# Rows 2 to 6 loaded in four 32-partition transfers, rows 0 to 6 stored in two 64-partition transfers

## The chip, the cores and the metric

The kernel runs on one core of a Trainium2 chip. The metric is device time in microseconds (us) of one execution; lower is better. Three runs of the kernel before gave 107.68, 107.85 and 108.42 us, so the median is 107.85 us. The core has five engines: PE (TensorE, matmul), DVE (VectorE), ACT (ScalarE), POOL (GpSimd) and SP (SyncE, which here only issues transfers and waits). Sixteen DMA engines move data between HBM, the memory outside the core, and SBUF, the core's working memory of 128 partitions.

## What is computed

The reference is windowed attention followed by a low-rank mixture of experts on the attention's output:

```
q, k, v: (8, 8, 576, 64) float32      # batch, heads, positions, head dim
scores = q k^T / 8
heads 0-3 keep 0 <= i-j < 32
heads 4-7 keep 0 <= i-j < 128 and (i-j) % 4 == 0
x = softmax(scores) v                 # then laid out as (8*576, 512)
logits = x @ w_gate                   # 512 -> 8 experts, the best two are taken, softmax of the two
out = x + sum over those two e of  w_e * (x @ A[e]) @ B[e]     # rank 16
```

All inputs and the output are float32; the kernel computes the matmuls in bfloat16 with float32 sums.

## The kernel before

A "row" here is one batch entry, r from 0 to 7. Each row has two groups g of four heads: the plain window and the dilated one.

**Data of a row.** One input slot `IN[r % 4]` holds q, k and v of a row in bfloat16 over 128 partitions; there are four slots, so row r+4 can only be loaded once row r's scores (operations `S...`) and value products (`V...`) have read their slot. Heads are packed in pairs, one of a pair in partitions 0 to 63 (half 0), the other in 64 to 127 (half 1). Each half of a row is a run of `ROW` = 6948 elements per partition, and the two halves start at different columns of the slot, with zeros in the rest. The result of a row is `X[r]`, 128 partitions x 2304 float32; each row has its own `X`, never reused.

**Loads.** They are issued from POOL (function `load`, line 248), because the transfer also turns float32 in HBM into bfloat16 in SBUF: an element is read as 4 bytes and written as 2. Every load names one half, that is 64 partitions. Rows 0, 1 and 7 come in several pieces so that their work can start early; rows 2 to 6 are one operation `L2` ... `L6` of two transfers, 64 partitions x 6948 elements each, and everything that uses the row waits for both:

```
a = load(f"L{r}", r, [(0, 0, ROW), (1, 2 * VB, ROW)], used.get(r - SLOTS, []))
```

**Work of a row.** For each group: scores and their mask on PE (`S`), exponentials on ACT (`E`, line 312), products with v on PE (`V`), reciprocal and division on DVE (`R` line 347, `N` line 350, which writes `X`), a bfloat16 copy on POOL (`B`, line 355). Then the experts: transposes on PE (`T`, `U`), copies, gate logits and first factor (`Z`), the top-two gates on DVE and ACT (`m0` to `g2`), scaling on POOL (`gz`, line 434), transposes (`G`), the second factor on PE (`D`) and its addition to `X` on DVE (`A`, lines 469 and 484).

**Stores.** They are issued from SP. Rows 0 to 6 are one transfer each of 128 partitions x 2304 float32 (line 496, operations `O0` to `O6`); row 7 goes in two transfers of 128 partitions x 1152, one per group (line 500, `O71` and `O70`). Each store waits for its row's additions and for a piece of row 7's load.

**Order.** The order of all operations is written out by hand in the text `PLAN`; each engine executes its own operations in that order. Semaphore waits are derived from the dependencies. An operation of several transfers has one semaphore, which counts 16 per transfer, and those who need it wait for all. Two rules are added for stores (lines 102 to 106): every store but the first waits for load `L71`, which is the last load to be issued, and a store of rows 0 to 6 waits for the store before the previous one, so that two are in flight:

```
if name[0] == "O":
    o.deps = o.deps + ([f"L{B - 1}1"] if stores else [])
    if int(name[1]) < B - 1:
        o.deps = o.deps + stores[-2:-1]
    stores.append(name)
```

The stores stand in the plan in the order `O1`, `O0`, `O3`, `O2`, `O4`, `O5`, `O6`, `O71`, `O70`.

The functions that the diff touches, with line numbers as the profile uses them:

Of the kernel before, what the change touches and what calls it, by code (L numbers as in the profile page):

```python
# [25 lines left out]
VB = 2 * NB * VW  # L26
ROW = 2 * (QK + VB)
SW = ROW + 2 * VB
XG = 1152
SLOTS = 4  # L30
# [44 lines left out]
class Program:  # L75
# [5 lines left out]
    def add(self, name, eng, work, emit, deps=(), bank=None):  # L81
        assert name not in self.ops, name
        o = Op(name, eng, work, emit, [d for d in deps if d is not None], bank)
        self.ops[name] = o
        if bank is not None:
            bank.users.append(name)
        return name
# [73 lines left out]
def program(nc=None, qkv=None, aw=None, bt=None, con=None, out=None):  # L161
    scale = 1.0 / float(D) ** 0.5
    pg = Program()
    add = pg.add

    def sb(name, shape, dt):
        return nc.alloc_sbuf_tensor(name, shape, dt) if nc is not None else None

    IN = [sb(f"in{i}", [128, SW], BF) for i in range(SLOTS)]
    X = [sb(f"x{r}", [128, 2 * XG], FP) for r in range(B)]  # L170
# [23 lines left out]
    def half(a):  # L194
        return slice(64 * a, 64 * a + 64)
# [45 lines left out]
    qk_ready, v_ready = {}, {}  # L241
    used = {}

    def load(name, r, parts, deps):

        def emit():
            return [
                nc.gpsimd.dma_start(  # L248
                    out=IN[r % SLOTS][half(a), at : at + n],
                    in_=qkv[r, a, :, at - 2 * VB * a : at - 2 * VB * a + n],  # L250
                )
                for a, at, n in parts
            ]

        return add(name, "POOL", ("dma", sum(64 for _ in parts), sum(4 * n for _, _, n in parts) // len(parts), len(parts)), emit, deps)

    def loads(r):
        if r == 0:
            for g in range(2):
                a = load(f"Lk{r}{g}", r, [(h, QK_AT[h][g], QK) for h in range(2)], [])  # L260
                b = load(f"Lv{r}{g}", r, [(h, V_AT[h][g], VB) for h in range(2)], [])
                qk_ready[r, g], v_ready[r, g] = [a], [b]
        elif r in (1, B - 1):
            free = used.get(r - SLOTS, [])
            a = load(f"L{r}0", r, [(0, VB, VB + QK), (1, 2 * VB + QK, VB + QK)], free)
            qk = [(0, 2 * VB + QK, QK), (1, 2 * VB, QK)]
            v = [(0, 0, VB), (1, ROW + VB, VB)]
            qk_ready[r, 0] = v_ready[r, 0] = [a]
            if r == 1:
                qk_ready[r, 1] = v_ready[r, 1] = [load(f"L{r}1", r, qk + v, free)]  # L270
            else:
                qk_ready[r, 1], v_ready[r, 1] = [load(f"L{r}1", r, qk, free)], [load(f"L{r}2", r, v, free)]
        else:
            a = load(f"L{r}", r, [(0, 0, ROW), (1, 2 * VB, ROW)], used.get(r - SLOTS, []))
            for g in range(2):
                qk_ready[r, g] = v_ready[r, g] = [a]

# [210 lines left out]
    for r in range(B):  # L488
        loads(r)
        for g in range(2):  # L490
            attention(r, g)
        used[r] = [f"S{p}{r}{g}" for p in range(2) for g in range(2)] + [f"V{r}{g}" for g in range(2)]
        adapters(r)
    for r in range(B):
        if r < B - 1:
            add(f"O{r}", "SP", ("dma", 128, 9216), lambda r=r: [nc.sync.dma_start(out=out[r], in_=X[r][:, :])],
                [f"A{r}{n}" for n in range(3)] + [f"L{B - 1}0"])
        else:
            for g in range(2):
                add(f"O{r}{g}", "SP", ("dma", 128, 4608), lambda r=r, g=g: [nc.sync.dma_start(  # L500
                    out=out[r][:, XG * g : XG * g + XG], in_=X[r][:, XG * g : XG * g + XG])],
                    [f"A{r}{g}", f"A{r}2", f"L{B - 1}0"])
# [92 lines left out]
```

## Time and profile before

| | us |
|---|---|
| median of three runs | 107.85 |
| the profiled execution's own time | 108.36 |
| its span, first to last instruction | 106.6 |
| PE busy | 83.0 |
| DVE busy | 73.2 |
| ACT busy | 56.7 |
| POOL busy | 44.6 |

The transfers wrote 24.68 MB at their destinations, a mean of 232 GB/s over the span. The page divides the span into 40 slices of 2.67 us; for each it gives the busy share of every engine in tenths, the granted clock of PE, the mean busy share of the 16 DMA engines and the rate. A rate counts the bytes as written; since the row loads read 4 bytes for 2 written, their reading rate is twice the rate shown. "Issue to landing" is the time from the instruction that issues a transfer until its semaphore shows it done, so it includes the wait behind other transfers. Sizes in KB are 1024 bytes; rates in GB/s are 10^9 bytes per second.

### The profile page before, as it was taken

The page shows a single profiled execution, that of the slowest core. Times are in us where ns is not written, and L with a number is a line of the kernel's source. Part 1 is how long each engine was busy: PE and PEld are TensorE (multiplying, and loading weights), DVE is VectorE, ACT ScalarE, POOL GpSimd, SP SyncE. Part 2 cuts the span into 40 slices and gives each one's busy share as a digit, 9 for nine tenths or more (in the row PEclk, how much of TensorE's full clock was granted, in tenths as well). Part 3 has the DMA queues.
Part 4 walks back from the last instruction along what each step waited for, and adds up shares of the span by engine and source line. Part 5 has one row for each costly group of instructions (what it writes and reads, how often), then busy time and mean ns, then how long its engine had stood idle before and what let it go on. Part 6 is the DMA issues. An engine that isn't in the chain of part 4 may idle for free.

```text
span 106.6 us, 3605 instructions
## 1 busy us (share of the span) xinstructions
PE 83.0 (78%) x1599; PEld 60.4 (57%) x1603; DVE 73.2 (69%) x167; ACT 56.7 (53%) x83; POOL 44.6 (42%) x59
## 2 busy tenths in 40 slices
PE   4999986799868768979739729999999998852700
PEld 1334662585647545868539517988887896621300
DVE  6772088187691794968319804899999799998630
ACT  0126603478529716765936918638896956650100
POOL 6999028307180177106643790047350945300000
PEclk9999999999999999999999995899999999998555
DMA  2999999999898999999999999936982999993982
GB/s 45 345 204 203 224 210 209 225 221 236 188 246 188 230 197 224 236 203 219 204 167 209 199 187 182 201 79 266 234 164 106 384 397 374 412 401 159 415 360 111
DMA packets 4142, 24.68 MB, mean 232 GB/s; under 512 B 672, under 2 KB 800, under 8 KB 2592
## 3 DMA queue, kind: packets, MB, share of 16 engines
q0 software_dynamic: 2400, 14.23, 66.3%
q1 hardware_dynamic: 1584, 9.95, 22.8%
q10 hardware_dynamic: 144, 0.28, 0.8%
q8 instruction: 12, 0.20, 0.7%
q14 instruction: 2, 0.02, 0.0%
HBM read 29.25 MB, written 9.44 MB: 363 GB/s over the span
## 4 chain that ended last, share of the span: by engine, by line
PE 31%; DMA 28%; DVE 19%; POOL 8%; issue 7%; ACT 2%; DVEq 1%; POOLq 0%
DMA in<-in_qkv_dram 28%; PE ps L204 26%; POOL in L248 8%; DVE x L469 6%; DVE x L350 5%; PE ps L371 4%; ACT p L312 1%; DVE x L484 1%; DVEq L586 1%; DVE gc L447 1%; DVE g L428 1%; PE ps L443 1%; DVE rec L347 1%; PE ps L390 1%; DVE gz L434 1%
## 5 line engine op out<-in xcount | busy, mean ns | idle before, releaser
L355 POOL CAST xb<-x 128x1152 bf16<-128x1152 f32 x16 | 19.7, 1229 | 31.5 <-DVE x L350 31.5
L312 ACT ACTIVATE p<-ps 128x960 bf16<-128x960 f32 (+1 forms) x32 | 27.5, 892 | 9.7 <-PE ps L204 9.6
L204 PE MATMUL ps<-in,p 128*64 128x130 bf16 (+1 forms) x416 | 21.4, 221 | 4.0 <-issue 3.0
L469 DVE TENSOR_TENSOR x<-x,ps 128x1024 f32<-128x1024 f32 x16 | 19.4, 1216 | 6.4 <-PE ps L204 6.3
L350 DVE TENSOR_TENSOR x<-ps,rec 128x1152 f32<-128x1152 f32 x16 | 21.7, 1354 | 0.4
L204 PEld LDWEIGHTS ps<-in,p 128*64 128x64 bf16 (+1 forms) x416 | 17.4, 104 | 7.5 <-issue 3.5
L248 POOL DMA_DIRECT2D in<-in_qkv_dram x30 | 15.9, 584 | 0.8 <-POOLq L577 0.8
L434 POOL TENSOR_TENSOR gz<-zs,g 128x640 bf16<-128x640 f32 x7 | 8.9, 1275 | 14.5 <-DVE g L428 14.3
L204 PE MATMUL ps<-in 64*64 64x96 bf16 (+1 forms) x576 | 12.0, 205 | 2.6 <-issue 2.6
L204 PEld LDWEIGHTS ps<-in 64*64 64x64 bf16 x576 | 11.1, 110 | 5.1 <-issue 3.0
L204 PE MATMUL ps<-con 64*64 64x384 bf16 (+1 forms) x128 | 12.2, 372 | 1.8 <-DMA in<-in_qkv_dram 1.3
L204 PE MATMUL ps<-warm 128*128 128x512 bf16 x39 | 11.6, 446 | 2.1 <-DVE warm L208 1.5
L383 ACT COPY xt<-ps 128x1024 bf16<-128x1024 bf16 x8 | 8.1, 1016 | 7.7 <-PE ps L371 7.7
L347 DVE RECIPROCAL rec<-ps 128x18 f32<-128x18 f32 x16 | 4.2, 266 | 11.4 <-PE ps L204 11.4
L371 PE MATMUL ps<-con,xb 128*128 128x128 bf16 x128 | 10.1, 225 | 1.5 <-POOL xb L355 1.4
L204 PE MATMUL ps<-aw,xt 128*128 128x136 bf16 x160 | 11.2, 223 | 0.0
L380 ACT COPY xt<-ps 128x1024 bf16<-128x1024 bf16 x8 | 8.1, 1014 | 5.2 <-PE ps L371 5.1
L415 ACT COPY zs<-ps 128x408 f32<-128x408 f32 (+1 forms) x16 | 6.9, 446 | 6.6 <-PE ps L204 6.5
L204 PEld LDWEIGHTS ps<-aw,xt 128*128 128x128 bf16 x160 | 9.6, 98 | 0.6
L371 PEld LDWEIGHTS ps<-con,xb 128*128 128x128 bf16 x128 | 8.0, 101 | 3.1 <-POOL xb L355 2.7
L239 DVE MEMSET in<- 64x1170 uint32 x8 | 8.3, 1033 | 2.1 <-issue 2.1
L449 ACT COPY gn<-ps 128x576 bf16<-128x576 bf16 x8 | 5.1, 640 | 7.1 <-DVE gc L447 6.9
(33 smaller groups left out, 70.6 us busy)
## 6 DMA issues: line engine op xcount, KB each, us to landing
in<-in_qkv_dram POOLq DMA_DIRECT2D x10, 868.5 KB, 15.8
out_dram<-x SPq DMA_DIRECT2D x7, 1152.0 KB, 5.7
in<-in_qkv_dram POOLq DMA_DIRECT2D x8, 288.0 KB, 7.1
in<-in_qkv_dram POOLq DMA_DIRECT2D x4, 434.2 KB, 9.9
in<-in_qkv_dram POOLq DMA_DIRECT2D x8, 146.2 KB, 8.2
out_dram<-x SPq DMA_DIRECT2D x2, 576.0 KB, 2.9
awf<-in_aw_dram ACTq DMA_DIRECT2D x1, 272.0 KB, 3.7
btf<-in_bt_dram SPq DMA_DIRECT2D x1, 256.0 KB, 3.7
```

The costliest lines, as they stand in the source:

```text
L204: return nc.tensor.matmul(o, lhsT=lhsT, rhs=rhs, start=start, stop=stop, skip_group_check=True)
L239: add(f"vz{i}{a}", "DVE", ("zero", 1170), lambda i=i, a=a: [nc.vector.memset(zeros(i, a), 0)])
L248: nc.gpsimd.dma_start(out=IN[r % SLOTS][half(a), at : at + n], in_=qkv[r, a, :, at - 2 * VB * a : at - 2 * VB * a + n],)
L312: return [nc.scalar.activation(p[:, :, :].rearrange("p h (s c) -> p h s c", c=PER)[:, :, b0 : b0 + nb, 0:SEG], PS[:, k.at : k.at + 2, 0 : ...
L350: nm = add(f"N{tag}", "DVE", ("el", XG), lambda: [nc.vector.tensor_tensor(X[r][:, XG * g : XG * g + XG].rearrange("p (b i n) -> p b i n", ...
L355: add(f"B{tag}", "POOL", ("el", XG), lambda: [nc.gpsimd.tensor_copy(XB[r % 2][:, g], X[r][:, XG * g : XG * g + XG])], [nm] + ([f"T{r - 2}{ ...
L371: nc.tensor.transpose(tp[:, 512 * j + 128 * u : 512 * j + 128 * u + 128], xb[:, g, 256 * u + 128 * j : 256 * u + 128 * j + 128], ident())
L380: return [nc.scalar.copy(xt[:, 0:2, 0:S].rearrange("p j (c i) -> p j c i", c=C)[:, :, :, 0:128], tp.rearrange("p j (i c) -> p j c i", c=C))]
L383: return [nc.scalar.copy(xt[:, 2:4, 0:512], tp)]
L415: zc.append(add(f"Y{st}{r}", "ACT", ("el", len(us) * ZW), lambda us=us, k=k: [nc.scalar.copy(zs[:, us[0] : us[-1] + 1].rearrange("p u n -> ...
L434: return [en.tensor_tensor(GZ[i][:, :, :].rearrange("p u (e r) -> p u e r", e=E), zs[:, :, 0:ER].rearrange("p u (e r) -> p u e r", e=E), G ...
L469: return [nc.vector.tensor_tensor(v, v, PS[:, k.at : k.at + 2].rearrange("p b n -> p (b n)"), ALU.add)]
```

## The change

The function that emits loads takes a width `cut` in partitions. With 32, each half of a row is loaded by two transfers, of partitions 0 to 31 and 32 to 63 of the half. This is used for rows 2 to 6 only, so ten transfers become twenty. Each store of rows 0 to 6 becomes two transfers, partitions 0 to 63 and 64 to 127; seven transfers become fourteen. The two stores of row 7 stay as they are. Bytes, waits and the order of operations on every engine stay the same; the pieces of one operation are issued one after the other and share its semaphore.

```
-    def load(name, r, parts, deps):
+    def load(name, r, parts, deps, cut=64):
 
         def emit():
             return [
                 nc.gpsimd.dma_start(
-                    out=IN[r % SLOTS][half(a), at : at + n],
-                    in_=qkv[r, a, :, at - 2 * VB * a : at - 2 * VB * a + n],
+                    out=IN[r % SLOTS][64 * a + p : 64 * a + p + cut, at : at + n],
+                    in_=qkv[r, a, p : p + cut, at - 2 * VB * a : at - 2 * VB * a + n],
                 )
-                for a, at, n in parts
+                for a, at, n in parts for p in range(0, 64, cut)
             ]
...
-            a = load(f"L{r}", r, [(0, 0, ROW), (1, 2 * VB, ROW)], used.get(r - SLOTS, []))
+            a = load(f"L{r}", r, [(0, 0, ROW), (1, 2 * VB, ROW)], used.get(r - SLOTS, []), 32)
...
         if r < B - 1:
-            add(f"O{r}", "SP", ("dma", 128, 9216), lambda r=r: [nc.sync.dma_start(out=out[r], in_=X[r][:, :])],
+            add(f"O{r}", "SP", ("dma", 128, 9216, 2), lambda r=r: [nc.sync.dma_start(out=out[r][half(a)], in_=X[r][half(a), :]) for a in range(2)],
                 [f"A{r}{n}" for n in range(3)] + [f"L{B - 1}0"])
```

## The prediction

> **What bounds the kernel now.** I read first the page's slices of the span, because the change touches only transfers, and its table of transfers.
>
> ```profile
> span 106.6 us, 3605 instructions
> ...
> PEclk9999999999999999999999995899999999998555
> DMA  2999999999898999999999999936982999993982
> GB/s 45 345 204 203 224 210 209 225 221 236 188 246 188 230 197 224 236 203 219 204 167 209 199 187 182 201 79 266 234 164 106 384 397 374 412 401 159 415 360 111
> ...
> out_dram<-x SPq DMA_DIRECT2D x7, 1152.0 KB, 5.7
> ```
>
> The transfer engines are busy in nearly every slice, in two stages of unlike speed: up to slice 26 (69 us) row loads, written at about 210 GB/s; from slice 31 (82 us) stores, at about 400 GB/s. A store of a row is 1152 KB, 1.18 MB. Next, the chain that ended last, in order of time (start, length), and the issues of SP's queue (start, length, count).
>
> ```profile
> 9.97 29.96 DMA in<-in_qkv_dram
> ...
> 60.51 2.65 issue
> ...
> 99.40 1.22 DVE x L469
> 100.62 0.33 DVE x L484
> 100.95 1.13 DVEq L586
> ```
> ```profile
> 81.30 0.82 SPq L496 DMA_DIRECT2D out_dram<-x  x2
> ```
> ```profile
> 97.92 0.33 SPq L496 DMA_DIRECT2D out_dram<-x  x1
> ```
> ```profile
> 100.97 1.47 SPq L500 DMA_DIRECT2D out_dram<-x  x2
> ```
>
> Up to 40 us the chain is the load stream, then it is compute, and it ends with DVE's last addition to row 7, after which the last piece `O70` goes out at about 102.1. So the store stream is not late today: `O6` goes out at 97.92, when its row's last addition is through, not because a transfer held it. What keeps the stores from starting earlier is `L71`:
>
> ```profile
> SPq L496 <- DMA in<-in_qkv_dram: 79.3, 2, 70.7
> ```
>
> ```profile
> 72.27 0.35 SPq L496 DMA_DIRECT2D out_dram<-x  x1
> ```
>
> SP waits 70.7 us for `L70`, issues `O1` at 72.3, and waits the other 8.6 us for `L71`, which lands at 81.3 with the issue of `O0`. Between 81.3 and the end, six rows and row 7 (8.26 MB) must leave. The windows show what room that has (the last two columns: DMA share and GB/s).
>
> ```profile
> 24.00:32.00 8.00, 6.43 (x128) 4.35 (x129) 6.52 (x12) 4.71 (x7) 4.59 (x5) 1.00 1.05 223
> 32.00:54.00 22.00, 17.25 (x448) 13.62 (x441) 13.87 (x35) 15.35 (x23) 8.76 (x10) 1.00 1.01 213
> 82.00:87.50 5.50, 5.50 (x116) 4.73 (x113) 4.92 (x9) 4.13 (x7) 3.12 (x3) 1.00 1.02 420
> 88.00:97.00 9.00, 6.15 (x76) 4.34 (x75) 8.92 (x31) 4.82 (x10) 2.43 (x2) 1.00 0.94 393
> 102.00:104.00 2.00, 0.00 (x0) 0.00 (x0) 0.08 (x1) 0.00 (x0) 0.00 (x0) 0.50 1.03 424
> ```
>
> At 393 to 424 GB/s one row takes 2.8 to 3.0 us, and the whole stage is full already (share 0.94 to 1.03). There is little slack: whatever makes a store's row much slower than 3 us turns the store stream into the bound.
>
> **The change part by part.** *Issue of ten more loads on POOL.* The group of the loads, and the instructions that follow them on POOL, with their idle time in brackets:
>
> ```profile
> L248 POOL DMA_DIRECT2D in<-in_qkv_dram x30 | 15.9, 584 | 0.8 <-POOLq L577 0.8
> ```
> ```profile
> 15.28 1.14 POOL L355 CAST xb<-x 128x1152 bf16<-128x1152 f32 x1 [4.62 <-DVE x L350]
> ...
> 37.02 1.27 POOL L434 TENSOR_TENSOR gz<-zs,g 128x640 bf16<-128x640 f32 x1 [5.42 <-DVE g L428]
> ...
> 47.87 1.15 POOL L355 CAST xb<-x 128x1152 bf16<-128x1152 f32 x1 [4.91 <-DVE x L350]
> ...
> 57.62 1.14 POOL L355 CAST xb<-x 128x1152 bf16<-128x1152 f32 x1 [3.14 <-DVE x L350]
> ```
>
> One issue costs 0.58 us, and the group's mean holds pieces of 146 to 869 KB, so I charge the same for half a piece: 10 x 0.58 = 5.8 us of POOL. They fall as 2.3 us behind `L2` and `L3`, ahead of an idle 4.62 us; and 1.2 us each behind `L4`, `L5` and `L6`, ahead of 5.42, 4.91 and 3.14 us. Nothing else stands between, so compute waits for none of it. Were that cover gone, the price would be those 5.8 us. The data do not run dry either, since `L2` to `L5` are issued well ahead of their turn in the stream; of `L6` (53.4) the last two quarters go out 1.2 us later, while its first two take 4 us to move. I take 0.
>
> *The loads themselves.* The halves of `L4`, with their issue on POOL and their landing:
>
> ```profile
> 30.49 1.11 POOL L248 DMA_DIRECT2D in<-in_qkv_dram  x2
> ```
> ```profile
> in<-in_qkv_dram POOLq DMA_DIRECT2D x1, 868.5 KB, 13.6
> ```
> ```profile
> in<-in_qkv_dram POOLq DMA_DIRECT2D x1, 868.5 KB, 17.4
> ```
>
> Issued at 30.49 and 0.57 later, they land at 44.1 and 48.5, one after the other, 4.4 us apart for 0.889 MB (204 GB/s): a transfer of half the partitions uses the whole DMA capacity while it lasts, and the next one follows. Four quarters in a row then move the same bytes. What a piece costs beside its bytes I bound by slices 2 to 6 (5.3 to 18.7 us), where some 12 small pieces of rows 0 and 1 flow: mean 210 GB/s against 223 with large pieces, 6% of 13.3 us, 0.8 us or 0.07 us a piece. Over ten pieces that is 0 to 0.7 us; the slices scatter by more, and from 32 to 54 us large pieces run at 213 too, so I take 0. Less than nothing is excluded, as the engines are at share 1.0 already. The Trainium skill, page "SBUF — State Buffer", section "Door 1: The DMA port swizzle", says that a span of 32 partitions reaches as many of SBUF's ports as one of 64, with 189 against 196 GB/s measured there; by that the five rows would take some 4% longer, an estimate of 1.6 us, mostly covered. No run here shows a 32-partition transfer.
>
> *The stores.* Issuing: seven more at 0.33 us (the row of 97.92), on an SP that otherwise waits: 0. The transfer is the term that counts. No uncast store of 64 partitions is in this trace, so I bound its rate from the nearest rows: 424 GB/s by kind (a store, but over 128 partitions), 213 to 223 GB/s by span (64 partitions, but a converting load). I take the row nearest by span, for one reason: width of span is what the change alters, and every 64-partition stretch in the trace, whatever its piece size, stays near 220 on the SBUF side, whereas 128-partition ones reach twice that. The halves of one store cannot make it up by running side by side if they behave as `L4`'s halves do. The same section of the Trainium skill states the rule that speaks against this change: partitions 0 to 63 reach only half of the ports, an asymptote of 218 against 436 GB/s, and two transfers on the two halves serialize. The load rows agree with 218, but the conversion would explain them too; by the rule a row's store takes 1.18/0.218 = 5.4 us, an estimate, and the sum would be the one below.
>
> With the mean of 223 and 213, 218 GB/s, a row takes 1.18 MB / 218 = 5.4 us. Now the path:
>
> ```profile
> out_dram<-x SPq DMA_DIRECT2D x1, 1152.0 KB, 4.1
> ```
> ```profile
> out_dram<-x SPq DMA_DIRECT2D x1, 576.0 KB, 3.0
> ```
>
> `O6` (4.1 us from issue to landing, with nothing behind it for most of the time) spends 1.18/0.424 = 2.8 us on data and 1.3 us on issue and landing. `O70`, issued at 102.1, lands at 105.1, so 1.5 us of the span follow.
>
> 1. `O1`, alone from 72.3, is 2.6 us slower and shares the engines with `L71`. `L71` lands later by nothing to 2.6 us; I take 1.5, so `O0` goes out at 82.8 in place of 81.3.
> 2. Six rows back to back: 6 x 5.4 = 32.4 us. Two stores are in flight always, so the wait for the one before the previous one leaves no gap (its cover is a 5.4 us transfer).
> 3. Row 7's two pieces, unchanged in form, are ready long before and queue behind: 1.18/0.424 = 2.8 us.
> 4. End of the span: 82.8 + 1.3 + 32.4 + 2.8 + 1.5 = 120.8 us.
>
> The profiled execution took 108.36 us for a span of 106.6, 1.8 us more, and it lies 0.5 us above the median. So 120.8 + 1.8 - 0.5 = **122 us**, 14 more than now. Compute has slack in it: `O6` would be issued when `O4` lands, at about 82.8 + 1.3 + 4 x 5.4 = 105.7, while its data are ready at 97.9 today and perhaps 2 us later then. With 204 and 223 GB/s for the rate, the six rows take 34.7 and 31.8 us; with `L71` later by 0 or 2.6, the outcome is 120 to 125.5. Lag between engines could save some: 118 to 126 is this case's own range.
>
> **The rivals.** *A, not slower: the rate belongs to the engine, not to the span.* Windows of the load stream's end:
>
> ```profile
> 68.50:69.00 0.50, 0.50 (x16) 0.41 (x12) 0.02 (x1) 0.50 (x2) 0.00 (x0) 1.00 1.09 222
> 70.50:71.00 0.50, 0.50 (x12) 0.50 (x10) 0.47 (x3) 0.00 (x0) 0.29 (x1) 1.00 0.28 56
> ```
>
> Per busy engine that is 222/(1.09 x 16) = 12.7 and 56/(0.28 x 16) = 12.5 GB/s: with a quarter of the engines at work, each is no faster. So a load is held within the engine, which reads 25 GB/s for these, about what one moves in the stores (424/(1.03 x 16) = 25.7). Then 220 GB/s is just half of 440 because of the conversion, says nothing on the span, and half-span stores run at 400. Sum: no term, 107.9 us, and 107.5 to 109 with what a piece costs. It decides if two engines that serve one half do not hold each other up. This speaks for A as regards loads, and is silent on stores; and it does not exclude a limit by span that lies at the same rate. A stays second because the trace has not one 64-partition stretch above 223 GB/s at the SBUF. [...]
>
> *B, half of the loss.* The rate halves only while engines on the same half move in step; where one lags by a few rows, the two halves overlap. The load stream's end drags over 2 us (a share of 0.28 at 70.5), so lag exists. At 300 GB/s a row takes 3.9 us: 6 x 3.9 = 23.6, and 82 + 1.3 + 23.6 + 2.8 + 1.5 = 111.2, or 112.5 us on the median's footing.
>
> *C, the loads halve as well.* If a quarter-span load ran at half of a half-span's rate, rows 2 to 6 would take 16 in place of 8.2 us each, on a path that waits for them: 39 us more on top, about 160. Only the fall from 128 to 64, if real, hints at it.
>
> *D, faster.* The chain holds 2.65 us at 60.51 in which PE waits for nothing shown, after which its clock falls (the slices' 5). If other lengths of pieces shift that stall away, and A holds, up to 4 us go: 104. Nothing in the trace ties it to piece length.
>
> **How the numbers follow.** Forecast 0.75, A 0.12, B 0.08, C 0.02, D 0.03. The range takes the forecast's own 118 to 126 and reaches down over B to 110; A and D (0.15), C and a little of the forecast stay outside. Within 1% is about what a measurement of this kernel can tell from no change: A gives most of it, 0.10; slower gets the rest of A, B, C and the forecast, 0.87; faster D, 0.03.
>
> **What would show it.** Right: the slices from 83 us on at about 220 GB/s with a DMA share still near 1; pieces of 576 KB on SP that land in 5 to 11 us; SP's wait for earlier stores growing to over 20 us; the chain ending in transfers out, with DVE done some 15 us before; POOL's idle times shorter by 1.2 to 2.3 us behind the loads; loads still near 215 GB/s up to 69 us. Wrong: stores at 400 GB/s in halves (A), or near 300 (B); loads near 110 (C); `L71` landing beyond 84.

## The result

The changed kernel takes 111.8 us (median of 4 runs, 110.86 to 114.92) against 108.1 us for the kernel before (4 runs), a ratio of 1.0315 with a 95% interval of 1.0225 to 1.0406. It is slower, as forecast, but by 3.7 us and not by 14. Some executions run disturbed, at a lower granted clock; the ratios leave them out, and of kernel e7 below one undisturbed run of 114.87 us remains, while its profile is of a disturbed one. The profiled execution took 112.14 us for a span of 110.4.

The page of the changed kernel, the same lines as for before:

```profile
span 110.4 us, 3622 instructions
...
DMA  3999999999899999999999998659999899999991
GB/s 56 327 214 203 219 220 200 218 245 217 186 243 212 192 240 207 202 237 207 199 186 212 200 151 167 123 84 266 262 314 310 294 273 277 354 331 241 249 347 62
...
L248 POOL DMA_DIRECT2D in<-in_qkv_dram x40 | 20.4, 571 | 0.8 <-POOLq L577 0.8
...
out_dram<-x SPq DMA_DIRECT2D x16, 576.0 KB, 6.3
```

The load stage, the first 24 slices, looks as it did. The store stage now stands at 241 to 354 GB/s where 360 to 415 were usual before, at a DMA share that is as full as then: the engines are busy, but get less through. By windows (last columns: clock, DMA share, GB/s):

```profile
24.00:32.00 8.00, 6.46 (x132) 4.40 (x129) 6.52 (x12) 4.57 (x7) 4.86 (x6) 1.00 1.06 223
32.00:54.00 22.00, 17.24 (x457) 13.70 (x445) 14.04 (x36) 15.70 (x23) 10.58 (x14) 1.00 1.01 213
84.00:96.00 12.00, 9.48 (x133) 7.22 (x132) 10.51 (x33) 6.64 (x13) 3.63 (x4) 1.00 0.99 296
```

Loads run at 223 and 213 GB/s, to the digit as before; stores at 296. The queue's line for 84 to 96 us (packets, MB, share of 16 engines), first of the kernel before, then of the changed one, turns this into the time of one packet, the 9216 bytes that a store takes from one partition:

```profile
q1 hardware_dynamic: 576, 4.72, 94.1%
```
```profile
q1 hardware_dynamic: 476, 3.52, 97.7%
```

Before: 0.941 x 16 x 12 us of engine time over 4.72 MB / 9216 B = 512 packets, 0.353 us each (the other 64 hold 4 bytes each). After: 0.977 x 192 us over 382 packets, 0.49 us. The loss is in the time that an engine takes for a packet. Where it shows at the end: `O70`, issued at 102.4, nearly as before (102.1), lands 7.0 us later, where 3.0 did before.

```profile
out_dram<-x SPq DMA_DIRECT2D x1, 576.0 KB, 7.0
```

### The profile page after: what moved, and what is told of

Read it like the earlier page. It is cut to its first block, busy times and chain, and to the rows that moved or that the text cites. A ratio compares the mean times of both kernels' runs of the same rounds, so it can differ in the third digit from the quotient of the medians.

```text
span 110.4 us, 3622 instructions
## 1 busy us (share of the span) xinstructions
PE 82.1 (74%) x1599; PEld 60.4 (55%) x1603; DVE 73.1 (66%) x167; ACT 56.4 (51%) x83; POOL 49.1 (44%) x69
## 4 chain that ended last, share of the span: by engine, by line
PE 34%; DMA 26%; DVE 15%; POOL 10%; issue 7%; DVEq 1%; ACT 1%; POOLq 0%
PE ps L204 28%; DMA in<-in_qkv_dram 26%; POOL in L248 10%; DVE x L469 5%; PE ps L371 4%; DVE x L350 4%; DVE x L484 1%; PE ps L443 1%; PE ps L390 1%; DVEq L586 1%; DVE gc L447 1%; ACT p L312 1%; DVE rec L347 1%; DVE gz L434 1%; DVE s L422 1%
## 5 line engine op out<-in xcount | busy, mean ns | idle before, releaser
L204 PE MATMUL ps<-in,p 128*64 128x130 bf16 (+1 forms) x416 | 22.4, 226 | 5.5 <-issue 4.6
L204 PEld LDWEIGHTS ps<-in,p 128*64 128x64 bf16 (+1 forms) x416 | 18.1, 107 | 9.4 <-issue 5.3
L248 POOL DMA_DIRECT2D in<-in_qkv_dram x40 | 20.4, 571 | 0.8 <-POOLq L577 0.8
L204 PE MATMUL ps<-warm 128*128 128x512 bf16 x39 | 10.7, 420 | 2.1 <-DVE warm L208 1.5
```

Source lines behind the costliest of these rows:

```text
L204: return nc.tensor.matmul(o, lhsT=lhsT, rhs=rhs, start=start, stop=stop, skip_group_check=True)
L248: nc.gpsimd.dma_start(out=IN[r % SLOTS][64 * a + p : 64 * a + p + cut, at : at + n], in_=qkv[r, a, p : p + cut, at - 2 * VB * a : at - 2 * ...
```

## The experiments

Three readings are compared. Theory S: two engines that serve the same group of partitions hold each other up, and 0 to 63 (or 64 to 127) is such that every group has two engines on it. Rival L: the ten more loads. Rival N: the number of transfers, their issue and completion.

**e1 and e11, loads in quarters alone.** The changed kernel with its stores put back:

```
-            add(f"O{r}", "SP", ("dma", 128, 9216, 2), lambda r=r: [nc.sync.dma_start(out=out[r][half(a)], in_=X[r][half(a), :]) for a in range(2)],
+            add(f"O{r}", "SP", ("dma", 128, 9216), lambda r=r: [nc.sync.dma_start(out=out[r], in_=X[r][:, :])],
```

> Only rows 2 to 6 are loaded in quarters; stores as before. If the stores' span is the cause (theory S), the time is that of the kernel before, 107.5 to 109 us, and the store stage runs near 400 GB/s. If the ten more pieces on POOL's queue are the cause (rival L), 110 to 112 us, with L70 landing 1 to 2 us later than the 71 us of before.

Measured 107.76 us (median of 10 runs) beside 108.51 (25 runs) for the kernel before on the same chip; no ratio is on record for this pair. The store stage is back at its rate:

```profile
84.00:96.00 12.00, 9.86 (x144) 7.51 (x139) 11.83 (x36) 7.02 (x13) 4.54 (x4) 1.00 0.90 376
```

Rival L falls: SP's wait for `L70` is 70.1 us, no longer than before. As the median lay a little below, the same kernel was measured again in more rounds:

> The loads in quarters alone, stores as before, in more rounds, since the first comparison left open whether they gain 1% or nothing. Nothing: within 0.7% of the kernel before. A gain by the quarters: 0.5 to 1.5% faster, which would make this version the fastest of all.

108.08 us beside 109.05, ratio 0.9933 with an interval of 0.9838 to 1.0027, which holds no change. Whether cut loads gain half a per cent stays open; no cost of them shows.

**e2, stores in halves alone.** The reverse: `load` called without the 32.

> Only the stores of rows 0 to 6 are cut into halves of 64 partitions; loads as before. Theory S: 111 to 112.5 us, nearly all of the changed kernel's loss, with the store stage near 300 GB/s at a DMA share near 1. Rival L: 107.5 to 109 us.

112.9 us, a little above the 111 to 112.5 expected, ratio 1.0464 (1.036 to 1.0567): the stores carry the whole loss. The more telling view is its store stream by windows of 2 us. In this run the DMA engines were idle from 80 to 82, so all started `O0` together:

```profile
82.00:84.00 2.00, 2.00 (x46) 1.55 (x44) 0.57 (x2) 2.00 (x4) 0.77 (x2) 1.00 0.95 202
84.00:86.00 2.00, 2.00 (x43) 1.80 (x44) 2.00 (x5) 1.60 (x3) 0.81 (x1) 1.00 0.88 221
86.00:88.00 2.00, 2.00 (x43) 1.86 (x38) 1.97 (x3) 0.96 (x2) 1.14 (x1) 1.00 1.03 263
88.00:90.00 2.00, 1.82 (x27) 1.35 (x24) 1.97 (x11) 1.26 (x4) 1.15 (x1) 1.00 0.95 326
90.00:92.00 2.00, 1.46 (x19) 0.94 (x17) 2.00 (x7) 1.82 (x3) 1.28 (x1) 1.00 1.01 336
92.00:94.00 2.00, 1.71 (x26) 1.42 (x23) 1.97 (x8) 1.15 (x3) 0.00 (x0) 1.00 0.98 346
...
98.00:100.00 2.00, 1.66 (x12) 0.88 (x12) 1.29 (x2) 0.64 (x1) 0.00 (x0) 0.79 1.02 387
...
104.00:106.00 2.00, 0.00 (x0) 0.00 (x0) 0.00 (x0) 0.00 (x0) 0.00 (x0) 0.50 0.96 256
```

The stream begins at half of the usual 400 GB/s, about the rate that the prediction took for the whole of it, and climbs to 346 within 10 us, with nothing in the form of the stores that changes from one row to the next. It does not stay there: between 94 and 106 us the windows scatter from 256 to 387, at a DMA share near 1. In the changed kernel too the rate falls back late in the stream:

```profile
100.00:106.00 6.00, 1.04 (x6) 0.43 (x4) 2.35 (x3) 0.00 (x0) 0.00 (x0) 0.50 0.96 247
```

**e3, two transfers again, but by columns.** As e2, with each store cut as row 7's is:

```
+ lambda r=r: [nc.sync.dma_start(out=out[r][:, XG * g : XG * g + XG], in_=X[r][:, XG * g : XG * g + XG]) for g in range(2)]
```

> Loads as before; each store of rows 0 to 6 in two transfers again, but of 128 partitions x 1152 elements. Theory S (the span of partitions): 107.5 to 109 us at about 400 GB/s. Rival N (the number of transfers, their issue and their completion): 110 to 112 us near 300 GB/s, as with the halves by partitions.

108.04 us, ratio 0.9985 (0.9934 to 1.0035), and the store stage near 400 GB/s:

```profile
84.00:96.00 12.00, 10.84 (x182) 8.72 (x182) 10.86 (x34) 8.74 (x15) 5.62 (x5) 1.00 0.97 391
```

Twice the transfers and half the row length cost nothing: rival N falls.

**e4, 64 other partitions.** As e2, with only the source changed:

```
- in_=X[r][half(a), :]
+ in_=X[r][32:96, :]
```

> Loads as before; each store of rows 0 to 6 in two transfers of 64 partitions to the same two places in HBM as in the changed kernel, but both read partitions 32 to 95 of the row (the values of the other partitions are not stored, those of 32 to 95 twice). Sizes, counts, row length and destinations are those of the changed kernel, only the partitions read differ. Theory S in its exact form (what counts is how many engines read from the same group of partitions, and 0 to 63 is one group): about 400 GB/s and 107.5 to 109 us. If 64 partitions in a transfer are slow whichever they are, or the number of transfers counts: near 300 GB/s and 110.5 to 112.5 us.

108.18 us, ratio 1.0007 (0.9945 to 1.007), and the store stage by window and queue line:

```profile
84.00:96.00 12.00, 10.91 (x181) 8.62 (x178) 10.68 (x32) 8.78 (x16) 5.48 (x5) 1.00 0.92 381
```
```profile
q1 hardware_dynamic: 603, 4.53, 90.6%
```

0.906 x 192 / 492 packets = 0.354 us a packet, as before. Sixty-four partitions are not slow as such; 0 to 63 and 64 to 127 are, and 32 to 95 are not.

**e5 and e6, one piece at a time.** Each half as an operation of its own that waits for the piece before it to land:

```
-                    o.deps = o.deps + stores[-2:-1]
+                    o.deps = o.deps + stores[-1:]
...
+            for a in range(2):
+                add(f"O{r}{'ab'[a]}", "SP", ("dma", 64, 9216), lambda r=r, a=a: [nc.sync.dma_start(out=out[r][half(a)], in_=X[r][half(a), :])],
```

and in e6 the source `X[r][32:96, :]`.

> Stores in halves of 64 partitions as in the changed kernel (loads as before), but every half waits until the one before it has landed, so that the two halves of a row never overlap. Theory S with lag: a lone half runs at half rate, 0.59 MB / 218 GB/s = 2.7 us and 1.3 us of issue and landing, 4.0 us from issue to landing; the 300 GB/s of the changed kernel then come from overlap of the two halves. If 300 GB/s is simply what a half-span store runs at: 0.59/300 + 1.3 = 3.3 us. If the halves only hurt each other: 2.8 us, as O71 before, a piece of the same size over 128 partitions. In all cases the kernel as a whole gets much slower (118 to 140 us), since twelve pieces go one at a time.

> The same, one piece at a time, but both pieces of a row read partitions 32 to 95 (the values of the other partitions are not stored). Theory S: 2.7 to 2.9 us from issue to landing, as O71 before. If any 64 partitions are slow alone: 3.3 to 4.0 us.

Issue to landing of one piece, and the queue's line over ten pieces or so, of e5 (90 to 130 us) and then of e6 (90 to 118):

```profile
out_dram<-x SPq DMA_DIRECT2D x1, 576.0 KB, 4.5
```
```profile
q1 hardware_dynamic: 720, 5.31, 63.1%
```
```profile
out_dram<-x SPq DMA_DIRECT2D x1, 576.0 KB, 3.0
```
```profile
q1 hardware_dynamic: 727, 5.37, 45.4%
```

A lone half takes 4.5 us, a lone middle piece 3.0. A packet takes 0.631 x 640 / 576 = 0.70 us in e5 and 0.454 x 448 / 583 = 0.35 us in e6: exactly twice. (Both pieces land 0.2 to 0.5 us later than I had, so 1.6 us and not 1.3 lie around the data.) The whole kernels took 145.5 and 128.8 us, one execution each, the first a little above my 118 to 140. So a half alone does run at half rate, and the 300 GB/s of the changed kernel need something else.

**e9 and e10, one row at a time.** e2 and the kernel before, each with `stores[-1:]` in place of `stores[-2:-1]`, so that every row starts with all engines together:

> Stores in halves of 64 partitions, loads as before; a row's two halves are queued one right behind the other, but a row waits until the row before it has landed, so all engines start every row in step. If the rate climbs because engines fall out of step over several rows: every row runs near 215 to 240 GB/s, 5.0 to 5.5 us of data and 1.6 us around it, about 7 us a row. If two queued halves overlap at once: near 300 GB/s, 5.5 us a row.

> The kernel before with the same one row at a time: the base for the run beside it. 2.9 us of data and 1.3 to 1.6 us around it, 4.2 to 4.5 us a row, as O6 before (4.1).

SP's issues of the first half of successive rows in e9, then of successive rows in e10:

```profile
96.17 0.47 SPq L496 DMA_DIRECT2D out_dram<-x  x1
```
```profile
103.08 0.47 SPq L496 DMA_DIRECT2D out_dram<-x  x1
```
```profile
93.22 0.33 SPq L496 DMA_DIRECT2D out_dram<-x  x1
```
```profile
97.38 0.33 SPq L496 DMA_DIRECT2D out_dram<-x  x1
```

6.9 us a row against 4.2, again one execution each. From the first packet of a row to the last, the trace has 5.4 us in e9, 2.9 in e10, and 3.0 for one lone half in e5: two halves queued right behind each other gain only about a tenth over two lone ones when the engines start in step. The rate rises only where the stream is not brought back into step, as in e2's windows.

That the engines do fall out of step in e2 can be read from the landings. A transfer raises its semaphore sixteen times, as often as there are engines; I take it that each engine does so once. For the first transfer of each of the six stores from `O0` on, the first twelve of these come within 0.07 to 0.16 us in the kernel before, e3 and e4, and within 0.13 to 0.14 us in e9. In e2 they come within 0.15 us for `O0`, and within 1.0 to 1.2 us for the five behind it.

So it is shown that the rate rises in unbroken work with halves and not across rows with a common start, and, if each engine raises once, that the engines drift apart in the first case and not in the second. That the drift is what raises the rate is argued: once one engine of a pair is a few packets ahead, it would already be at the other half, on other partitions, and both would run freely. The profile doesn't say which engine moved which packet. It fits that packets come in two kinds. The trace's durations of all 896 packets of 9216 bytes:

```
                     under 400 ns   400 to 600   over 600
before                    883           11           2
changed kernel            491          140         265
e2, halves                581          128         187
e5, lone halves            65           15         816
e9, one row at a time     270           69         557
e6, lone middle           891            2           3
```

In the changed kernel most packets take the time of a free one and some 30% that of a contested one; fewer lie between. In e9, with its common starts, 62% take over 600 ns.

**e7 and e8, quarters.** As e2, each store in four transfers of 32 partitions, in two orders:

```
+ lambda r=r: [nc.sync.dma_start(out=out[r][p : p + 32], in_=X[r][p : p + 32, :]) for p in (0, 32, 64, 96)]   # e7
+ lambda r=r: [nc.sync.dma_start(out=out[r][p : p + 32], in_=X[r][p : p + 32, :]) for p in (0, 64, 32, 96)]   # e8
```

> Loads as before; each store of rows 0 to 6 in four transfers of 32 partitions, in the order 0, 32, 64, 96. Theory S with lag: the first two quarters share one group, the last two the other, so engines change group as seldom as with halves: 290 to 315 GB/s in the store stage and 111.5 to 114 us. If narrower is slower: 250 GB/s or less and over 115 us.

> The same four transfers of 32 partitions, in the order 0, 64, 32, 96: the group changes with every quarter, twice as often. Theory S with lag: engines that lag by a row or two then sit in the other group more of the time: 330 to 400 GB/s and 108 to 111 us. If the rate is a fixed property of narrow transfers: the same as in the order 0, 32, 64, 96, within 1%.

e7 took 114.87 us in the one run that can be used (118.22 in the median of four), e8 111.8 and 113.1 (113.55 in the median of four). With so few runs, this comparison is weaker than the others. The queue's lines, e7 from 84 to 104 us and e8 from 84 to 102:

```profile
q1 hardware_dynamic: 857, 5.29, 95.3%
```
```profile
q1 hardware_dynamic: 883, 5.41, 87.1%
```

A packet takes 0.953 x 320 / 574 = 0.53 us in e7 and 0.871 x 288 / 587 = 0.43 us in e8: the order of the very same pieces seems to matter, in the direction of the theory. Three expectations were missed. The rates are 265 and 301 GB/s (5.29 MB in 20 us, 5.41 in 18), below 290 and 330; the times lie above the 111.5 to 114 and 108 to 111 us that go with them; and e7 isn't like the halves (0.49 us in the changed kernel) but worse. e8's share of 87% says that its engines also idle between the short pieces. The landings, read as for e9, come within 0.56 to 0.69 us in e7 (`O0` to `O5`) and within 0.73 to 1.10 us in e8 from its second store of this stage on, so the engines of e7 are less out of step. Why they are was not tried, and stays open.

## Why the prediction was wrong

**The step that failed** is the second of the sum: "Six rows back to back: 6 x 5.4 = 32.4 us", at one rate throughout. The price of engines in step is right (e2 begins at 202 GB/s; a row of e9 has 5.4 us of data, as forecast), but I took it for the whole stream, on the premise that two halves cannot make it up side by side because `L4`'s did not. From issue of `O0` to the last landing I had 1.3 + 32.4 + 2.8 = 36.5 us; measured are 78.5 to 109.4, 30.9 us:

```profile
78.53 0.47 SPq L496 DMA_DIRECT2D out_dram<-x  x1
```

That is 5.6 us of the 10.4 by which the span came out shorter, but here `O1` still had 55 of its 128 packets to start when `O0` went out. In e2 all of `O1`'s packets had been started by then, so e2 gives the term by itself. The issue of `O0`, and the second half of `O6`, issued at 100.2:

```profile
81.37 0.47 SPq L496 DMA_DIRECT2D out_dram<-x  x1
```
```profile
out_dram<-x SPq DMA_DIRECT2D x1, 576.0 KB, 7.1
```

`O6` lands at 107.3, 25.9 us after the issue of `O0`. Less the 1.3 us, six rows take 24.6 us where the sum has 32.4: 4.1 us a row in place of 5.4, and 7.8 us too much in this one term. I had named the reason myself as rival B, lag at 300 GB/s and 112.5 us, and gave it 0.08; it came near the rate (296 in the window) and the time. Its 300 GB/s was assumed there and not worked out from a row, so that the number fits so well is in part luck. The row on which I could have built more: the drag of 2 us at the end of the load stream, which I quoted, was nearly six times the 0.35 us that a store's packet takes, and half of a store is only four packets for each engine.

**The first step, `L71`,** had the wrong sign in this execution. I let `O1` delay `L71` by 1.5 us; in fact `O0` went out at 78.5, not 82.8, which is 4.3 us of the 10.4. SP's waits tell how:

```profile
SPq L496 <- DMA in<-in_qkv_dram: 75.8, 2, 72.6
```

`L70` landed at 74.2, 2 us later than before, so `O1` was issued behind the last piece of `L71` and stood less in its way: SP waited 3.2 us for `L71` (75.8 - 72.6) in place of 8.6. The other runs bear this out. In the six profiles in which `O1` goes out behind `L71` (this one, e5, e6, e8, e9, e11), `L71` lands at 77.6 to 79.6; in the seven in which `O1`, or most of it, goes out ahead of that last piece, at 80.7 to 83.1. Loads in one piece and loads in quarters stand on both sides, so the earlier landing is the timing of one execution and no gain of the quarters. Nor did slower stores cost what I charged: in e2, with `O1` just ahead, `O0` went out at 81.4, as in the kernel before, so my 1.5 us were nothing there. The remaining 0.5 us are the end of the span, 1.0 in place of 1.5.

**POOL** was right. The idle times ahead of the instructions behind `L3`, `L4`, `L5` and `L6`:

```profile
15.41 1.14 POOL L355 CAST xb<-x 128x1152 bf16<-128x1152 f32 x1 [2.93 <-DVE x L350]
...
37.15 1.27 POOL L434 TENSOR_TENSOR gz<-zs,g 128x640 bf16<-128x640 f32 x1 [4.51 <-DVE g L428]
...
47.46 1.15 POOL L355 CAST xb<-x 128x1152 bf16<-128x1152 f32 x1 [3.46 <-DVE x L350]
...
57.79 1.14 POOL L355 CAST xb<-x 128x1152 bf16<-128x1152 f32 x1 [2.69 <-DVE x L350]
```

They shrank by 0.5 to 1.7 us and none ran out, so ten issues at 0.57 us cost nothing. **The loads** were right too: 213 to 223 GB/s in the same windows, and e1. That also answers rivals C and D: no load was slower, and no run shows a gain that is clear of noise. **Rival A** fell by e2 and e4: stores in halves do lose. Its reading of the loads (the engine holds them, by the conversion) may stand; no run here tests it.

**The rule of the Trainium skill**, page "SBUF — State Buffer", section "Door 1: The DMA port swizzle", that 0 to 63 reach half of the ports and 32 to 63 share theirs with 0 to 31, agrees with e5, e6 and e4 (0.70 us a packet, 0.35, 0.35): a factor of two. Its next section, "Can I just issue two DMAs to hit both halves?", and not the one that the prediction names, has the rule that they serialize: two such transfers gain 6% over one. A single pair here, in e9, gains about as little, a tenth. A stream of such pairs runs at 202 GB/s at first and at 296 to 306 in the window from 84 to 96 us (the changed kernel and e2), and there the measurement decides.

## What to carry to other kernels

A store that spans only partitions 0 to 63 or 64 to 127 doubled the time of each packet while the engines worked in step, from 0.35 to 0.70 us for 9216 bytes; if such a store has to be cut, cut columns (e3, no loss), or choose 64 partitions across the middle (e4, no loss). Cutting the converting loads from 64 to 32 partitions lost nothing that shows (e1, e11). When pricing a stream from the rate of one piece, ask whether the engines stay in step: here the conflict eased over some 10 us of unbroken work without going away (about 300 GB/s in place of 400), and it was back at the start of every row that all engines began together (e9).

## What was not expected

The rate of one unchanged stream of stores rose from 202 to 346 GB/s in 10 us (e2) and then scattered. Making such a stream wait for each row costs more than the waits: e9 pays 2.7 us a row more than e10, at equal waits. And the order alone of four equal pieces seems to have moved the time of a packet from 0.53 to 0.43 us (e7, e8).
